# Exponentials on VectorE beside a long convolution: a new rule for when the planner gives VectorE a unit of softmax

## The chip, the cores and the metric

The kernel runs on one core of one Trainium2 chip. The metric is the device time of one execution in microseconds; of several executions the median is given.

## The reference

Two independent branches are computed and laid side by side in the last dimension. Everything is in bf16, S = 2048 positions, D = 640 channels.

```python
# branch A, out[..., 0:640]
k_shift = sum over t of k_pad[:, t:t+S, :] * shift_k[:, ks-1-t]     # ks = 4
kv = k_shift * v
y  = causal convolution of kv with ssm_k along S (written as rfft, product, irfft)
y  = y + kv * ssm_D
a  = q * y
# branch B, out[..., 640:1280]
q, k, v = split(x @ wqkv) into 32 heads of 20
p = softmax(q @ k.T * 20 ** -0.5)
b = (p @ v) joined over heads @ wo
```

Branch B holds 32 heads x 2048 x 2048 = 134 million exponentials. Branch A holds a convolution of length 2048 in each of 640 channels, and after it three elementwise operations for each output: kv times ssm_D, plus y, times q.

## The kernel before

**Units.** The scores are made transposed, keys on the 128 partitions and 512 queries along the free dimension. One such 128x512 tile of one head is a *unit*; there are 2048 of them (NU), and four units (four heads, one block of keys) make a *block*. TensorE writes the scores of a unit into one of eight PSUM banks (`S_task`, the matmul in line 568), an engine takes the exponential and writes bf16 into a slot of `P_sb`, and TensorE multiplies by V (`PV_task`, line 646), block after block in order. The row sums come out of a column of ones in V.

**Two engines take exponentials.** ScalarE takes groups of three and two units in turn, one ACTIVATE for each group (line 585, `EXP_task`), from banks 0 to 4. VectorE can take one more unit after each group (`VEXP_task`, `vexp_iter`): its scores go to the bank called AUX, and five VectorE instructions make the exponential from integer and polynomial steps: lines 615, 618, 620, 623 and 625. The first step is put out at once, the other four wait in a list called `chain`, which holds two units at most. VectorE's units have four slots of `P_sb` of their own.

**A planner writes the order.** When the kernel is built, a loop (the `while nu[0] < NU` loop) walks through model time. It keeps a time `P.T` for each engine and a cost `c` for each instruction, and decides what TensorE does next: the next score group as soon as its banks come free, urgent work, a pair of PV blocks, a piece of convolution, other tasks, and, when nothing else can be put in, matmuls on zeros (`zeros`, line 317). Each engine then runs its instructions in the written order, and waits on semaphores. The planner's times exist only at build time: they settle the order, not the speed.

VectorE's list is filled at two places. `fill_dve(now)` runs at each turn of the loop and puts out steps as long as VectorE's model time is not past `now`:

```python
while P.T["dve"] <= now + 0.05 and dve_step(now):
```

and `P.gap` lets a VectorE instruction that would wait be preceded by such steps. `dve_step` serves `chain` first; only when it is empty does it serve the list `micro`, in which the VectorE work of branch A stands.

**Branch A in stages.** First `kv_iter` computes k_shift times v (118 steps on VectorE, lines 476, 485, 489 and 508) and stores kv to a scratch tensor in HBM. Then the convolution runs on TensorE as 40 block rows of 16 channels (`conv_iter`, line 869: 128 small matmuls each, 5120 in all). After each block row VectorE copies the result out of the bank MISC, splits off the rounding (lines 882, 883), TensorE adds shifted parts (line 890), and VectorE copies into `Y` (line 896). Five block rows make a *chunk* of 80 channels; there are eight chunks. When a chunk of the convolution is finished, `A_iter` is put on `micro`: it loads q and kv for the chunk, and does the three elementwise operations (line 913) for each of four parts h, 12 steps a chunk. Parts 0 and 1 are loaded at the start into two pairs of buffers; the loads of parts 2 and 3 are issued after the output of parts 0 and 1 has been sent from the same buffers. These transfers, the convolution's (four banks of rows of `kext`, `hk_load`, one load for a quarter of a block row, four ahead; and `kvx_load`), and the outputs are all issued on SyncE's queue (SP), in order.

**When VectorE may take a unit** is settled in `vec_at`, asked once for every ScalarE group. It refuses when two units are in `chain`, when VectorE's model time is over 1.1 us ahead, when the slot has not been read, when the AUX bank is not free, and by pace. During `kv_iter`, 0.9 steps per us counted from 60 us must have been done. Afterwards:

```python
elif micro and kv_done[0] < a_at[0] + 12 * (now - a_at[1]) / (20 if conv_over else 50):
    return False
elif not conv_over and conv_b < 40 * (n - CONV0) / (NU - CONVE - CONV0):
    return False
```

So as long as steps of `A_iter` are left, they must have kept a pace of 12 in 50 us from the end of the chunk, or VectorE gets no unit. The second condition asks that the convolution keep pace with the units: `conv_b` block rows begun, n units begun, 40 block rows at n = 2008.

## Time and profile before

| | |
|---|---|
| median of 5 executions | 901.09 us (900.52 to 903.14) |
| profiled execution, its own time | 903.14 us |
| its span, first to last instruction | 901.3 us |
| ScalarE (ACT) busy | 882.7 us, 98% |
| TensorE (PE) busy | 866.6 us, 96% |
| VectorE (DVE) busy | 610.0 us, 68% |
| units taken by ScalarE, by VectorE | 1940, 108 |

The page names engines PE (TensorE matmuls), PEld (its weight loads), DVE (VectorE), ACT (ScalarE), POOL (GpSimd) and SP (SyncE, which here only issues transfers). A group's line gives source line, engine, operation, output and input, shapes, how many (x), then busy time in us and the mean ns of one, then the engine's idle time just before them and what ended it. Sums of steps are made against the profiled execution; 1.84 us of its own time lie outside the span.

The stages by time: projections and the start of attention to about 75 us; `kv_iter` beside attention to about 207 us; the convolution's matmuls from 233.5 to 852.7 us, with the eight chunk ends (last copy into `Y`) at 312.7, 394.7, 469.1, 547.3, 624.9, 708.4, 786.7 and 855.7 us; the last exponential ends at 892.55 us and the rest is the end of branch B.

### The profile page before, as it was taken

How to read it: one execution, taken by the hardware profiler on the slowest of the kernel's cores; microseconds unless marked ns; L12 is line 12 of the kernel's file. 1: busy time of each engine (PE TensorE's matmuls, PEld its weight loads, DVE VectorE, ACT ScalarE, POOL GpSimd, SP SyncE). 2: the span in 40 equal slices, each digit the busy share in tenths (PEclk: the TensorE clock that was granted, in tenths of full speed). 3: DMA queues.
4: the chain of work that ended last, by engine and by line, in shares of the span. 5: the costliest groups of instructions: out<-in, count | busy, mean ns of one | idle time of the engine just before them, and what ended most of it. 6: DMA issues, size and time to landing. Idle time of an engine off the chain costs nothing.

```text
span 901.3 us, 26290 instructions
## 1 busy us (share of the span) xinstructions
PE 866.6 (96%) x11636; PEld 406.2 (45%) x11636; DVE 610.0 (68%) x1142; ACT 882.7 (98%) x788; POOL 51.7 (6%) x75
## 2 busy tenths in 40 slices
PE   9999999999999999999999999999999999999997
PEld 5433322222455445455555455454545545455522
DVE  3477677677777777767775775777577475857741
ACT  6999999999999999999999999999999999999996
POOL 3001224332000000000000000000000000000000
PEclk9999999999999999999999999999999999999999
DMA  9512367766867668858866875895687677658410
GB/s 288 171 41 72 119 195 231 219 192 130 183 157 169 162 141 179 176 159 183 185 159 167 199 167 146 182 208 140 143 201 157 183 173 176 169 144 203 109 30 30
DMA packets 175517, 144.98 MB, mean 161 GB/s; under 512 B 138769, under 2 KB 150155, under 8 KB 175403
## 3 DMA queue, kind: packets, MB, share of 16 engines
q1 hardware_dynamic: 164027, 129.60, 59.1%
q0 software_dynamic: 9920, 13.33, 5.7%
q8 instruction: 91, 1.49, 0.7%
q10 hardware_dynamic: 1456, 0.37, 0.2%
q14 instruction: 23, 0.19, 0.1%
HBM read 124.67 MB, written 21.09 MB: 162 GB/s over the span
## 4 chain that ended last, share of the span: by engine, by line
ACT 96%; PE 4%; DVE 0%; issue 0%; DVEq 0%
ACT P_sb L585 96%; PE PS L392 1%; PE PS L568 1%; PE PS L317 1%; PE PS L447 0%; PE PS L646 0%; PE PS L368 0%; PE PS L749 0%; DVE P_sb L793 0%; DVE OT_sb L655 0%; DVEq L1182 0%; PE PS L670 0%; PE PS L772 0%; DVE V_sb L453 0%; DVE KT L380 0%
## 5 line engine op out<-in xcount | busy, mean ns | idle before, releaser
L585 ACT ACTIVATE P_sb<-PS 128x1024 bf16<-128x1024 f32 (+1 forms) x780 | 878.1, 1414 | 4.4 <-PE PS L568 4.2
L568 PE MATMUL PS<-QT,KT 20*128 20x512 bf16 x2048 | 303.8, 385 | 27.4 <-ACT P_sb L585 23.1
L869 PE MATMUL PS<-R 128*128 128x128 bf16 (+15 forms) x5120 | 249.6, 193 | 1.1 <-DVE R L896 1.1
L869 PEld LDWEIGHTS PS<-R 128*128 128x128 bf16 x5120 | 199.1, 96 | 105.5 <-issue 105.4
L568 PEld LDWEIGHTS PS<-QT,KT 20*128 20x128 bf16 x2048 | 74.8, 91 | 223.3 <-ACT P_sb L585 166.9
L646 PE MATMUL PS<-P_sb,V_sb 128*21 128x512 bf16 x2048 | 155.0, 383 | 0.9 <-DVE P_sb L625 0.7
L615 DVE TENSOR_SCALAR XI<-PS 128x512 int32<-128x512 f32 x108 | 74.6, 691 | 73.4 <-PE PS L568 72.0
L625 DVE SCALAR_TENSOR_TENSOR P_sb<-XZ,XI 128x512 uint16<-128x512 f32 x108 | 74.6, 690 | 3.0
L618 DVE SCALAR_TENSOR_TENSOR XZ<-XI 128x512 f32<-128x512 uint16 x108 | 74.3, 688 | 2.1
L317 PE MATMUL PS<-Zt 128*128 128x512 bf16 x252 | 74.7, 392 | 1.0 <-DVE Zt L311 1.0
L620 DVE SCALAR_TENSOR_TENSOR XZ<-XZ,XI 128x512 f32<-128x512 f32 x108 | 74.1, 686 | 1.6
L476 DVE TENSOR_TENSOR R<-R 128x640 bf16<-128x640 bf16 (+1 forms) x96 | 57.8, 602 | 2.0 <-DMA R<-in_A_v_dram 0.2
L646 PEld LDWEIGHTS PS<-P_sb,V_sb 128*21 128x21 bf16 x2048 | 30.8, 89 | 56.5 <-issue 48.3
L192 POOL DMA_DIRECT2D kvm_scratch<-R x64 | 43.9, 692 | 143.7 <-DVE R L508 142.3
L623 DVE TENSOR_SCALAR XI<-XI 128x512 int16<-128x512 int16 x108 | 49.3, 456 | 2.0
L655 DVE CAST OT_sb<-PS 128x512 bf16<-128x512 f32 x32 | 22.1, 689 | 39.2 <-PE PS L646 39.2
L380 DVE CAST QT<-PS 128x512 bf16<-128x512 f32 (+1 forms) x32 | 21.9, 684 | 36.8 <-PE PS L392 36.8
L380 DVE CAST KT<-PS 128x512 bf16<-128x512 f32 (+1 forms) x32 | 21.7, 678 | 29.5 <-PE PS L392 29.4
L392 PE MATMUL PS<-xT,R 128*20 128x512 bf16 (+2 forms) x660 | 41.5, 381 | 0.0
L392 PE MATMUL PS<-xT,WQ 128*20 128x512 bf16 (+1 forms) x660 | 40.3, 374 | 0.0
L882 DVE CAST ZH<-PS 128x256 bf16<-128x256 f32 x40 | 16.9, 423 | 22.4 <-PE PS L869 22.2
L453 DVE CAST V_sb<-PS 128x160 bf16<-128x160 f32 (+1 forms) x48 | 18.4, 383 | 17.2 <-PE PS L447 16.5
(51 smaller groups left out, 359.6 us busy)
## 6 DMA issues: line engine op xcount, KB each, us to landing
R<-kext_scratch SPq DMA_DIRECT2D x640, 132.0 KB, 3.1
kvm_scratch<-R POOLq DMA_DIRECT2D x64, 160.0 KB, 5.5
R<-kvm_scratch SPq DMA_DIRECT2D x32, 320.0 KB, 5.1
R<-in_A_k_dram SPq DMA_DIRECT2D x15, 640.0 KB, 3.8
kext_scratch<-in_A_ssm_k_dram POOLq DMA_DIRECT2D x1, 2560.0 KB, 13.5
R<-in_A_v_dram SPq DMA_DIRECT2D x16, 160.0 KB, 4.3
kv_scratch<-R SPq DMA_DIRECT2D x16, 160.0 KB, 5.0
R<-in_A_q_dram SPq DMA_DIRECT2D x32, 80.0 KB, 2.5
```

The costliest lines, as they stand in the source:

```text
L317: P.op("pe", lambda e: e.matmul(bank[bk], Zt, zrhs, start=start, stop=start, skip_group_check=True), reads=[b_Zt], writes=[bkb[bk]], tok=s ...
L392: ins = e.matmul(bank[bk][32 * i:32 * i + DH, 0:n], Wt[:, cc, off + i * DH:off + (i + 1) * DH], xT[:, cc, x0:x0 + n], start=(cc == 0), sto ...
L476: P.op("dve", lambda e: e.tensor_tensor(o, a, b, op), reads=reads, writes=writes, c=c)
L568: ins = e.matmul(bank[b], KT[32 * u:32 * u + DH, g, kb * 128:(kb + 1) * 128], QT[32 * u:32 * u + DH, qs(qc, g), :], start=True, stop=True, ...
L585: P.op("act", lambda e: e.activation(P_sb[:, s0:s0 + k, :], PS[:, b0 * 512:(b0 + k) * 512].rearrange("p (u q) -> p u q", u=k), ACT.Exp, sc ...
L615: step(lambda e: e.tensor_scalar(XI, bank[bk], scale * 1.4426950408889634 * w, 127.0 * w, op0=ALU.mult, op1=ALU.add), [bkb[bk]], [bi])
L618: step(lambda e: e.scalar_tensor_tensor(XZ, u, w * c2 / c3, u, op0=ALU.add, op1=ALU.mult), [bi], [bz])
L620: step(lambda e: e.scalar_tensor_tensor(XZ, XZ, w * w * c1 / c3, u, op0=ALU.add, op1=ALU.mult), [bi, bz], [bz])
L623: step(lambda e: e.tensor_scalar(hi, hi, 128.0, None, op0=ALU.mult), [bi], [bi])
L625: step(lambda e: e.scalar_tensor_tensor(P_sb[:, slot[n], :].bitcast(U16), XZ, 128.0 * c3 / w ** 3, hi, op0=ALU.mult, op1=ALU.add), [bi, bz ...
L646: ins = e.matmul(bank[OBANK][32 * u:32 * u + DH + 1, :], V_sb[:, kb, 4 * g + u, :], P_sb[:, slot[4 * b + u], :], start=(kb == 0), stop=(kb ...
L869: P.op("pe", lambda e, o=o, lhsT=lhsT, rhs=rhs, st=st, last=last: e.matmul(o, lhsT, rhs, start=st, stop=last, skip_group_check=True), read ...
```

## The change

The buffers for branch A's elementwise part become four pairs, and `A_iter` issues all four pairs of loads at its start. The pace of 12 steps in 50 us is replaced by a count: `a_at` is now the number of steps that would be done if all finished chunks were, and `vec_at` refuses a unit only when more than BACK = 12 steps are outstanding, or when the convolution is over and any are. `fill_dve` puts out steps up to 0.35 us ahead of VectorE's model time. Two costs in the planner's book change: the fourth step of a VectorE unit (line 623) from 0.7 to 0.48, and a step of `A_iter` from 0.43 to 0.33. No instruction of the kernel is changed in itself; what changes is order, and how many units go to which engine. The region R in SBUF, in which these buffers lie, is as large as before, since its other use (24,960 elements a partition) is larger than the new need (23,808).

```diff
+BACK = 12
...
-        ph1 = NHK * HK_E + 2 * KVX_E + 2 * Y_E + 4 * AST_E
+        ph1 = NHK * HK_E + 2 * KVX_E + 2 * Y_E + 8 * AST_E
...
-        Aq = [carve(AST_E).rearrange("p (t c) -> p t c", t=4) for _ in range(2)]
-        Akv = [carve(AST_E).rearrange("p (t c) -> p t c", t=4) for _ in range(2)]
+        Aq = [carve(AST_E).rearrange("p (t c) -> p t c", t=4) for _ in range(4)]
+        Akv = [carve(AST_E).rearrange("p (t c) -> p t c", t=4) for _ in range(4)]
...
-            def step(fn, reads, writes):
-                P.op("dve", fn, reads=reads, writes=writes, c=0.7)
+            def step(fn, reads, writes, c=0.7):
+                P.op("dve", fn, reads=reads, writes=writes, c=c)
...
-            step(lambda e: e.tensor_scalar(hi, hi, 128.0, None, op0=ALU.mult), [bi], [bi])
+            step(lambda e: e.tensor_scalar(hi, hi, 128.0, None, op0=ALU.mult), [bi], [bi], 0.48)
...
         def A_load(B, h):
-            i = h % 2
+            i = h
...
         def A_iter(B):
-            A_load(B, 0)
-            A_load(B, 1)
+            for h in range(4):
+                A_load(B, h)
...
-                P.op("dve", lambda e: e.tensor_tensor(o, a, b, op), reads=reads, writes=writes, c=0.43)
+                P.op("dve", lambda e: e.tensor_tensor(o, a, b, op), reads=reads, writes=writes, c=0.33)
...
-                if h + 2 < 4:
-                    A_load(B, h + 2)
...
-            while P.T["dve"] <= now + 0.05 and dve_step(now):
+            while P.T["dve"] <= now + 0.35 and dve_step(now):
...
-        kv_done, a_at = [0], [0, 0.0]
+        kv_done, kv_base, a_at = [0], [0], [0]
...
-            elif micro and kv_done[0] < a_at[0] + 12 * (now - a_at[1]) / (20 if conv_over else 50):
+            elif micro and (conv_over or a_at[0] - kv_done[0] > BACK):
+
                 return False
...
-            if not micro:
+            if not micro and not kv_over:
                 kv_over = True
+            if kv_over and not kv_base[0]:
+                kv_base[0] = kv_done[0]
...
-                            a_at[:] = [kv_done[0], P.T["pe"]]
+                            a_at[0] = max(a_at[0], kv_base[0]) + 12
```

## The prediction

> **What bounds the kernel.** I read the chain that ended last first, then the costliest groups, then waits, then stages.

> ```profile
> ACT 96%; PE 4%; DVE 0%; issue 0%; DVEq 0%
> ...
> L585 ACT ACTIVATE P_sb<-PS 128x1024 bf16<-128x1024 f32 (+1 forms) x780 | 878.1, 1414 | 4.4 <-PE PS L568 4.2
> ...
> L615 DVE TENSOR_SCALAR XI<-PS 128x512 int32<-128x512 f32 x108 | 74.6, 691 | 73.4 <-PE PS L568 72.0
> ```

> ScalarE's exponentials are the whole path, and it idles 4.4 us before them. So the time is 1940 units at 878.1 / 1940 = **0.453 us** each, plus the two ends. A unit moved to VectorE saves 0.453 us as long as TensorE keeps up. On VectorE the five groups of lines 615 to 625 are busy 346.9 us for 108 units: 3.21 us each. VectorE has idle time, and much of it is before line 615: it waits for the scores of a unit that the planner has given it late. The question is how many more units the new rules give it.

> The stages show where units are missing. Rows are stretch, its length, line 615's busy time and count, then TensorE's clock, DMA share and GB/s:

> ```profile
> 395.00:445.00 50.00, 4.14 (x6) 1.00 0.79 169
> 445.00:469.00 24.00, 3.94 (x6) 1.00 0.84 194
> ...
> 708.00:758.00 50.00, 2.77 (x4) 1.00 0.75 177
> 758.00:787.00 29.00, 4.84 (x7) 1.00 0.74 178
> ```

> The longer stretches run from a chunk's end to its last step of line 913, where the pace rule holds. Over the seven of them before 855 us (341 us) VectorE takes 40 units and is busy 229 us, 67%; over the eight others from 225 us (289 us) 63 units, busy 217.5 us, 75%. VectorE's order after the chunk end at 394.7 us shows the mechanism:

> ```profile
> 398.93 0.69 DVE L625 SCALAR_TENSOR_TENSOR P_sb<-XZ,XI 128x512 uint16<-128x512 f32 x1
> 404.47 0.69 DVE L655 CAST OT_sb<-PS 128x512 bf16<-128x512 f32 x1 [4.84 <-PE PS L646]
> ...
> 408.76 0.32 DVE L913 TENSOR_TENSOR R<-R,Dbc 128x320 bf16<-128x320 bf16 x1
> ...
> 411.64 0.69 DVE L615 TENSOR_SCALAR XI<-PS 128x512 int32<-128x512 f32 x1 [1.25 <-PE PS L568]
> ```

> Units are refused from the chunk's end, the queued ones drain, only then are loads issued (402.18 us on SP's queue), and no unit starts for 18.8 us (392.80 to 411.64). Parts 2 and 3 repeat it: loads at 414.49, next step at 424.80.

> **Loads and buffers.** The same 64 transfers, four pairs in a row instead of two. Two pairs took SP from 402.18 to 404.26 us, so four take 4.2 us, ahead of the convolution's loads, which stand up to three quarter rows ahead; a block row comes every 15.6 us (607.9 us for 39), so three quarters are 11.7 us. Hidden. Removed are SP's waits for the output to leave a buffer, 40.8 us in 16; these hide nothing today, since line 869 waits 1.1 us in all. Price of both: 0; if the cover were gone, 4.2 us a chunk on TensorE. A new load of part 3 can wait behind the previous chunk's output only where two chunks run back to back; about 2.6 us (40.8 / 16), under the same cover.

> **Pace rule.** If the seven stretches ran like the others, VectorE would be busy 0.753 x 341 = 257 us instead of 229: 28 us, or +8.6 units.

> **Looking ahead, and the booked costs.** Today a step is put out only when the book shows VectorE free, and the loop turns only once per piece of TensorE work: 0.39 us for a score group, 0.61 for a PV pair, 1.26 for a projection. A step that comes due inside a piece waits half of it. With these pieces filling roughly 33%, 18% and 5% of the stage, that is 0.06 + 0.055 + 0.03 = 0.15 us; less the 0.05 allowed, 0.1 a step, 0.5 a unit. The booking of line 623 adds 0.22. So up to 0.7 of the 1.13 us that VectorE idles per unit in the free stretches (71.5 us / 63) is the book's, not the chip's.

> [...] a step starts 0.72 us after the one it reads from (busy 0.69), and 0.61 after one it doesn't. [...] But the idle time before lines 618 to 625 is only 8.7 us for 108 units; what the lookahead shortens lies ahead of line 615, in the book. I take the book, at part.

> **Sum for 225 to 855 us.** VectorE is busy 447 us there, 103 units x 3.21 = 331 and 116 other. In about 620 us at a busy share y it takes (620 y - 116) / 3.21 units: y = 0.753 gives 109 (+6), 0.84 gives 126 (+23), 0.92 gives 141 (+38). Copies that wait for TensorE in VectorE's own order stay (lines 380, 882, 896, 655 and 715 wait 90 us here), so I take 0.84. Before 225 us units are rationed by `kv_iter`'s pace: by 95 us 19 steps are done where 31 are asked. A quicker book catches up late: +3 (0 to +8). The **convolution's pace** takes some back. At 855.7 us, when it ends, ScalarE has (892.55 - 855.7) / 0.453 = 81 units left, so n is about 1967 where 2008 is allowed: room for 41 units, less 2.2 (1 / 0.453) for each us that it ends later. Steps put out ahead stand before the two VectorE copies of each block row; 0.15 us a row, 6 us in all, leave 28. TensorE can carry it: it is busy 96%, but 100 matmuls on zeros lie in this stage (about 26 us), and 14 us of gaps. I take -4. Together **+22 units, -10.0 us**: 893.1 for an execution like the profiled one, **891** against the median of 901.09 (901.1 - 10.0). The last chunk's steps ended at 874.4 us, 18 us before ScalarE did; today's end is unchanged, and up to 24 steps (24 x 0.35 = 8.4 us) still fit.

> **Rivals.** *More*: the convolution keeps its speed and VectorE reaches 0.9: +31 to +48 units, 879 to 887. For it: decisions in the free stretches are frequent, one per ScalarE group (1.13 us). Against: the 90 us of copies.
> *Starved steps*: `chain` is served first, and if it is never empty the steps of a chunk wait until the next one ends; units are then refused until a chunk's loads and 12 steps are through, about 6 us (402.18 to 408.76) and 4. Seven times 10 us are 70 us, 22 units at worst; half of that leaves +4 to +15: 894 to 899.
> *Nothing*: the copies and TensorE's order fix VectorE's share: 899.3 to 902.9.
> *Slower*: TensorE waits in order for a VectorE unit. One place shows the price; rows are TensorE's busy time in 1 us stretches with its clock, then ScalarE:

> ```profile
> 94.00:95.00 1.00, 0.72 (x7) 1.00 0.00 0
> 95.00:96.00 1.00, 0.58 (x6) 0.70 0.00 0
> 96.00:97.00 1.00, 1.00 (x14) 0.50 0.78 271
> ...
> 99.14 4.62 ACT L585 ACTIVATE P_sb<-PS 128x1536 bf16<-128x1536 f32 x4 [1.52 <-PE PS L568]
> ```

> PV waited 0.70 us for line 625, a projection then ran at half clock (2.35 us instead of 1.26), ScalarE lost 1.52 us. [...] Here gaps of 0.70 and 0.44 us within 3 us were enough, [...] by the row 1.5 us each. It happened once with 108 units. From seven (10.0 / 1.52) it eats the gain; with ten to fourteen more the time is 906 to 912. Against it: with the looser book VectorE reached line 615 before its scores nearly always (72 us of waiting), and that margin shrinks but does not vanish.

> **How the numbers follow.** +16 to +30 units, 887.5 to 894: 0.54. More: 0.12. Starved: 0.21. Nothing: 0.05. Slower: 0.08. This kernel's measurement can tell about 0.2%, 899.3 to 902.9. Faster 0.54 + 0.12 + 0.21 = 0.87, same 0.05, slower 0.08. The range 883 to 899 leaves out about 0.07 below and 0.13 above; it holds the likeliest case whole.

> **What would show it.** Line 615 counts about 130, and line 585 some nine ACTIVATEs fewer; VectorE's share from 225 to 855 us rises from 71% to about 84%; no stretch of 15 us without a unit follows a chunk's end; loads of branch A come in fours; idle time before line 615 falls under 0.4 us each. If ScalarE's idle time before line 585 rises above 10 us, the slower rival is at work; if line 913 comes in blocks of 12 or more right after the next chunk's end, the starved one. I am wrong if the count moves by under ten, or if the time doesn't follow it at 0.45 us a unit.

## The result, and the profile after

The changed kernel takes 889.88 us in the median of 25 executions (887.68 to 905.77), against 901.08 before (900.28 to 903.32); the ratio is **0.9888, interval 0.9876 to 0.9901**. I had forecast 891. The median holds some executions in which TensorE's clock fell: of 26 listed with their clock, 17 had 0.998 or more and lie between 887.7 and 892.1 us, nine had 0.979 to 0.996 and lie between 892.3 and 905.8. Line numbers in the changed kernel are one higher from here on (615 is 616).

The page of the changed kernel, span 887.5 us, own time 889.33: the chain by engine, then ScalarE's exponentials and the first step of a VectorE unit, with busy time, mean ns and idle time before.

```profile
ACT 92%; PE 4%; DMA 1%; SPq 1%; DVE 0%; issue 0%; DVEq 0%
...
L586 ACT ACTIVATE P_sb<-PS 128x1024 bf16<-128x1024 f32 (+1 forms) x769 | 865.2, 1416 | 3.7 <-PE PS L569 3.6
...
L616 DVE TENSOR_SCALAR XI<-PS 128x512 int32<-128x512 f32 x137 | 94.7, 691 | 33.3 <-PE PS L569 29.0
```

VectorE takes 137 units instead of 108, ScalarE 1911 in 769 ACTIVATEs instead of 780, and ScalarE is busy 12.9 us less (878.1 to 865.2): 0.445 us a unit. ScalarE still has the path, and waits no more than before. Idle time ahead of line 616 fell from 0.68 to 0.24 us each. New in the chain are a transfer and SP's queue, 1% each.

All engines in the stage from 225 to 855 us; busy time and count of PE, PEld, DVE, ACT, POOL, then clock, DMA share, GB/s:

```profile
225.00:855.00 630.00, 611.32 (x9045) 317.58 (x9042) 529.88 (x979) 629.25 (x558) 0.00 (x0) 1.00 0.70 166
```

VectorE is busy 529.9 of 630 us, 84.1%, where it was 446.8. But the stage is not even. Line 616 by stretches (busy time, count):

```profile
294.00:368.00 74.00, 11.06 (x16) 1.00 0.67 170
368.00:384.00 16.00, 0.81 (x2) 1.00 0.67 156
384.00:449.00 65.00, 10.26 (x15) 1.00 0.82 184
449.00:464.00 15.00, 0.86 (x2) 1.00 0.38 103
```

and VectorE's order in the second of them:

```profile
368.17 0.69 DVE L616 TENSOR_SCALAR XI<-PS 128x512 int32<-128x512 f32 x1
...
372.31 0.42 DVE L897 CAST R<-PS 128x256 bf16<-128x256 f32 x1
...
375.94 0.32 DVE L914 TENSOR_TENSOR R<-R,Dbc 128x320 bf16<-128x320 bf16 x1
...
381.40 0.69 DVE L914 TENSOR_TENSOR R<-R 128x320 bf16<-128x320 bf16 x2
383.88 0.69 DVE L616 TENSOR_SCALAR XI<-PS 128x512 int32<-128x512 f32 x1 [1.79 <-PE PS L569]
```

The chunk that ended at 294.0 us gets none of its 12 steps until the next one ends at 372.3. Then units are refused, the steps run in one block, and 15.7 us pass without a new unit (368.17 to 383.88). The same happens at each later chunk end. Between the blocks a unit starts every 4.3 to 4.6 us (65 / 15 and 74 / 16) where the mean of this stage was 6.2 before (630 / 102).

### The profile page after: what moved, and what is told of

Its sections match the earlier page's. It is cut to its first block, busy times and chain, and to the rows that moved or that the text cites. A ratio compares the mean times of both kernels' runs of the same rounds, so it can differ in the third digit from the quotient of the medians.

```text
span 887.5 us, 26392 instructions
## 1 busy us (share of the span) xinstructions
PE 850.1 (96%) x11594; PEld 402.5 (45%) x11594; DVE 697.8 (79%) x1287; ACT 869.7 (98%) x777; POOL 51.7 (6%) x75
## 4 chain that ended last, share of the span: by engine, by line
ACT 92%; PE 4%; DMA 1%; SPq 1%; DVE 0%; issue 0%; DVEq 0%
ACT P_sb L586 92%; PE PS L393 1%; DMA R<-kvm_scratch 1%; SPq L193 1%; PE PS L569 1%; DMA R<-kext_scratch 1%; PE PS L318 1%; PE PS L750 0%; PE PS L647 0%; PE PS L448 0%; PE PS L369 0%; DVE P_sb L794 0%; PE PS L870 0%; DVE OT_sb L656 0%; DVEq L1184 0%
## 5 line engine op out<-in xcount | busy, mean ns | idle before, releaser
L586 ACT ACTIVATE P_sb<-PS 128x1024 bf16<-128x1024 f32 (+1 forms) x769 | 865.2, 1416 | 3.7 <-PE PS L569 3.6
L569 PE MATMUL PS<-QT,KT 20*128 20x512 bf16 x2048 | 299.0, 384 | 28.8 <-ACT P_sb L586 24.6
L616 DVE TENSOR_SCALAR XI<-PS 128x512 int32<-128x512 f32 x137 | 94.7, 691 | 33.3 <-PE PS L569 29.0
L626 DVE SCALAR_TENSOR_TENSOR P_sb<-XZ,XI 128x512 uint16<-128x512 f32 x137 | 94.6, 690 | 4.0
L621 DVE SCALAR_TENSOR_TENSOR XZ<-XZ,XI 128x512 f32<-128x512 f32 x137 | 94.2, 687 | 2.6
L619 DVE SCALAR_TENSOR_TENSOR XZ<-XI 128x512 f32<-128x512 uint16 x137 | 93.8, 685 | 1.4
L624 DVE TENSOR_SCALAR XI<-XI 128x512 int16<-128x512 int16 x137 | 62.9, 459 | 3.5
L318 PE MATMUL PS<-Zt 128*128 128x512 bf16 x210 | 63.2, 392 | 1.0 <-DVE Zt L312 1.0
L448 PE MATMUL PS<-R,xT 128*128 128x160 bf16 (+1 forms) x240 | 29.1, 256 | 0.1
## 6 DMA issues: line engine op xcount, KB each, us to landing
kext_scratch<-in_A_ssm_k_dram POOLq DMA_DIRECT2D x1, 2560.0 KB, 13.9
```

What stands on the lines that cost most here:

```text
L318: P.op("pe", lambda e: e.matmul(bank[bk], Zt, zrhs, start=start, stop=start, skip_group_check=True), reads=[b_Zt], writes=[bkb[bk]], tok=s ...
L569: ins = e.matmul(bank[b], KT[32 * u:32 * u + DH, g, kb * 128:(kb + 1) * 128], QT[32 * u:32 * u + DH, qs(qc, g), :], start=True, stop=True, ...
L586: P.op("act", lambda e: e.activation(P_sb[:, s0:s0 + k, :], PS[:, b0 * 512:(b0 + k) * 512].rearrange("p (u q) -> p u q", u=k), ACT.Exp, sc ...
L616: step(lambda e: e.tensor_scalar(XI, bank[bk], scale * 1.4426950408889634 * w, 127.0 * w, op0=ALU.mult, op1=ALU.add), [bkb[bk]], [bi])
L619: step(lambda e: e.scalar_tensor_tensor(XZ, u, w * c2 / c3, u, op0=ALU.add, op1=ALU.mult), [bi], [bz])
L621: step(lambda e: e.scalar_tensor_tensor(XZ, XZ, w * w * c1 / c3, u, op0=ALU.add, op1=ALU.mult), [bi, bz], [bz])
```

## The experiments

**Which part brought the units.** My theory was that the time follows the number of units, and that the planner's book (look-ahead and booked costs) gives most of them; the rival was that only the pace rule counts (+8.6 units). The book alone, on the kernel before:

```diff
-            while P.T["dve"] <= now + 0.05 and dve_step(now):
+            while P.T["dve"] <= now + 0.35 and dve_step(now):
...
-            step(lambda e: e.tensor_scalar(hi, hi, 128.0, None, op0=ALU.mult), [bi], [bi])
+            step(lambda e: e.tensor_scalar(hi, hi, 128.0, None, op0=ALU.mult), [bi], [bi], 0.48)
...
-                P.op("dve", lambda e: e.tensor_tensor(o, a, b, op), reads=reads, writes=writes, c=0.43)
+                P.op("dve", lambda e: e.tensor_tensor(o, a, b, op), reads=reads, writes=writes, c=0.33)
```

> Kernel before with the look-ahead of 0.35 us and the booked costs (0.48 and 0.33) alone; old pace rule, two pairs of buffers. As planned, VectorE takes 134 units. Theory (units decide, and the planner's book gives them): 26 more units at 0.453 us are 11.8 us, so about 889.3 us. Rival [...]: within 2 us of before, 899 to 902 us. A third reading, that the trains of loads on SP's queue cause the spread of the changed kernel, expects this one's executions to lie within 4 us of each other.

Measured 890.68 us (890.09 to 897.71, four executions, ratio 0.9893, interval 0.9852 to 0.9935). Its page:

```profile
L585 ACT ACTIVATE P_sb<-PS 128x1024 bf16<-128x1024 f32 (+1 forms) x770 | 866.6, 1419 | 3.0 <-PE PS L568 2.8
...
L615 DVE TENSOR_SCALAR XI<-PS 128x512 int32<-128x512 f32 x134 | 92.5, 690 | 36.6 <-PE PS L568 33.4
```

26 of the 29 new units come from three numbers in the book. The third reading fails in one of its four executions, 7 us off (clock 0.990), in a kernel whose loads of branch A go out in fours and twos: a fall of the clock doesn't need the trains of eight. The look-ahead alone, the first of the three edits:

> Kernel before with the look-ahead of 0.35 us alone; as planned, 121 units. Theory (units decide): 13 units, 5.9 us less than before's undisturbed executions of 900.6, about 894.7 us. [...]

Measured 895.79 us (895.10 to 895.89), 121 units, ratio 0.9948 (0.9933 to 0.9962): 4.8 us for 13 units against executions of before on that chip at 900.56, where 5.9 were forecast. The rest, alone:

```diff
+BACK = 12
...
-            elif micro and kv_done[0] < a_at[0] + 12 * (now - a_at[1]) / (20 if conv_over else 50):
+            elif micro and (conv_over or a_at[0] - kv_done[0] > BACK):
...
+            for h in range(4):
+                A_load(B, h)
```

(with the four pairs of buffers and the counters that belong to it)

> Kernel before with the count in place of the pace rule and four pairs of buffers alone; old look-ahead and booked costs. As planned, 117 units. Theory (units decide): 9 more units, 4.1 us less, about 897.0 us. The rival [...] (this part carries the gain) expects most of the 11 us: 890 to 893 us.

Measured 902.29 us (898.17 to 915.59): both missed. It has its 117 units, and its lowest execution, 898.17, is near the 897.0 that they ask for; but 14 of 22 executions have a clock of 0.977 to 0.995, up to 17 us longer. So the count in place of the pace rule, with its buffers, is worth +9 units alone and +3 on top of the book, and brings something that costs more. What that is comes after one test of the units.

Is it the units at all, or does the new order save waits? One more refusal in the changed kernel:

```diff
+CAP = 108
...
-            if len(chain) > 1 or not 140 < n < NU - 30 or P.T["dve"] > now + 1.1:
+            if vn[0] >= CAP * (n - 140) / (NU - 170) or len(chain) > 1 or not 140 < n < NU - 30 or P.T["dve"] > now + 1.1:
```

> The changed kernel with one more refusal: VectorE gets no unit beyond an even share of 108 over the run. Everything else of the change stays. Theory (units alone decide): same count as before, 900 to 902 us. Rival (the new order saves waits of its own): under 898 us. Rival (the new order costs waits that the extra units hide): over 904 us.

Measured 901.53 us (900.44 to 912.40; one of 12 over 903), ratio 1.0008 (0.9985 to 1.0031). With the old count the new order has the old time, within 0.3%. The units decide.

**What halves the clock.** An execution of pace_only that took 915.05 us was profiled. Its order around 720 us, transfers, TensorE and ScalarE:

```profile
719.66 0.51 SPq L193 DMA_DIRECT2D R<-in_A_q_dram  x1
...
720.20 0.51 SPq L193 DMA_DIRECT2D R<-kv_scratch  x1
...
720.76 2.51 SPq L193 DMA_DIRECT2D R<-kext_scratch  x4
...
725.83 0.29 PE L870 MATMUL PS<-R 128*128 128x128 bf16 x2 [1.38 <-DMA R<-kext_scratch]
...
726.49 2.37 ACT L586 ACTIVATE P_sb<-PS 128x1536 bf16<-128x1536 f32 x2 [1.07 <-PE PS L569]
```

Eight loads of branch A stand in a row on SP's queue from 716.30 us; the convolution's rows, issued behind them, land late; TensorE waits 1.38 us in order at line 870. Then TensorE by stretches (busy, count, clock, DMA share, GB/s):

```profile
720.00:727.00 7.00, 5.60 (x95) 1.00 0.97 191
727.00:740.00 13.00, 13.00 (x97) 0.50 0.92 183
740.00:755.00 15.00, 15.00 (x167) 0.50 0.39 110
755.00:764.00 9.00, 9.00 (x56) 0.50 0.61 117
764.00:780.00 16.00, 15.90 (x233) 0.98 0.60 147
```

The clock is halved for 37.5 us by the trace's record, and ScalarE, which idles 17.5 us in this execution where 2.8 is usual, loses about 15 us. The theory is that the trains of eight loads make the convolution's loads late; the rival, that TensorE has too little work by itself. The trains alone are not enough: cap108 puts its loads out in trains of eight too, two of them 13.9 us apart (370.65 and 384.50 us), and only one of its 12 executions has a lower clock. Here the train began 14.2 us after the one before it (702.08 us). First I took the loads off SP's queue:

```diff
-            P.dmas("sp", [(Aq[i], ap(q2, dims, o)), (Akv[i], ap(kvd, dims, o))], d_aq[i],
+            P.dmas("pool", [(Aq[i], ap(q2, dims, o)), (Akv[i], ap(kvd, dims, o))], d_aq[i],
```

> The changed kernel with the loads of branch A's elementwise part issued on GpSimd's queue instead of SP's; as planned, 138 units. Theory (trains of eight loads on SP's queue delay the convolution's loads, TensorE waits, and in some executions its clock is halved): all executions within 3 us, granted clock 0.998 or above, median about 887.5 us. Rival (TensorE's work is too thin by itself, whatever the queue): executions spread over 5 us or more with clocks of 0.98 to 0.995 as in the changed kernel, whose executions go from 887.7 to over 899 us.

Measured 899.09 us (894.23 to 909.85), every one of 20 executions with a clock under 0.998: worse than the changed kernel. The timeline says why it was a poor test:

```profile
215.91 0.75 POOL L193 DMA_DIRECT2D R<-in_A_q_dram  x1
...
221.13 13.27 SPq L193 DMA_DIRECT2D R<-kext_scratch  x16
...
228.38 0.37 PE L870 MATMUL PS<-R 128*128 128x128 bf16 x2 [7.05 <-DMA R<-kvm_scratch]
...
230.30 1.02 ACT L586 ACTIVATE P_sb<-PS 128x1024 bf16<-128x1024 f32 x1 [7.28 <-PE PS L569]
```

On GpSimd's queue nothing stood ahead of the first chunk's loads, so they were issued from 213 us, among the first loads of the convolution, of which one then came 7 us late. In the changed kernel SP's order holds them back to 370.86 us. The clock is halved again behind a late load of the convolution (7.05 us of waiting, then 44.4 us at half clock), but this doesn't test the trains. That the early transfers delayed the convolution's is what the order suggests; it was not separated.

Better was to leave the queue and give the convolution's loads more lead, one bank of rows more, in the changed kernel and in pace_only:

```diff
-NHK = 4
+NHK = 5
```

> The count and the four pairs of buffers alone (old look-ahead and booked costs), with five banks of convolution rows; as planned, 116 units. With four banks half the executions lay between 908 and 916 us. Theory (late loads): none over 905 us, median 897 to 899 us (8 units at 0.453 are 3.6 us). Rival (want of work): still a good share over 905 us.

Measured 897.40 us (896.59 to 899.74), ratio 0.9970 (0.9961 to 0.9979), 116 units. None of nine executions has a clock under 0.998, where 14 of 22 had with four banks. ScalarE's row with four banks (the execution above), then with five:

```profile
L586 ACT ACTIVATE P_sb<-PS 128x1024 bf16<-128x1024 f32 (+1 forms) x777 | 876.3, 1409 | 17.5 <-PE PS L569 17.2
```

```profile
L586 ACT ACTIVATE P_sb<-PS 128x1024 bf16<-128x1024 f32 (+1 forms) x777 | 874.5, 1421 | 2.8 <-PE PS L569 2.7
```

For the count alone this shows late loads as the cause, as far as one chip can be set against another: the two ran on different chips, with 116 and 117 units. That it was the trains that made them late was not separated. In the changed kernel itself:

> The changed kernel with five banks of convolution rows instead of four (NHK = 5), so the convolution's loads are issued one quarter row (about 3.9 us) earlier. As planned, VectorE takes the same 137 units. Theory (trains of eight loads on SP's queue make the convolution's loads late, TensorE waits in order, its clock is halved for tens of us in some executions): TensorE's waits for kext go to nothing, granted clock 0.998 or above in nearly all executions, median 887 to 888.5 us, all under 892. Rival (the clock is halved for want of work on TensorE, not for late loads): a tail of executions from 892 to 906 us as in the changed kernel.

Measured 889.10 us (888.06 to 889.52), ratio 0.9871 (0.9859 to 0.9884), no wait for kext left (one of 0.5 us for `kvm_scratch` is). Four executions are few against a tail of one in three, so both kernels ran once more side by side:

> The changed kernel with five banks once more, for more executions beside the changed kernel on the same chip. Theory (late loads): again 887.5 to 890 us, none over 892. Rival (four executions were too few to see the tail): a third of them over 892, as with four banks.

> The changed kernel itself, for comparison on the same chip: 888 to 890 us in about two of three executions, the others 892 to 906 with a granted clock under 0.998.

Five banks: 889.07 us (888.33 to 903.82, one of four with a clock of 0.978). Changed kernel: 891.93 us (888.99 to 912.62, four of seven under 0.998). Together one of eight against 13 of 33. The direction is the theory's, but chance alone would give one or none of eight about one time in seven, and one execution at 903.82 went against "none over 892". There is a second cause that five banks don't remove, or the lead is still short in some executions. No trace of such an execution was taken, and this stays open.

**What the four pairs of buffers are for.** In the changed kernel, two pairs as before, part h + 2 loaded behind the output of part h:

```diff
-            i = h
+            i = h % 2
...
-            for h in range(4):
-                A_load(B, h)
+            A_load(B, 0)
+            A_load(B, 1)
...
+                if h + 2 < 4:
+                    A_load(B, h + 2)
```

> The changed kernel with two pairs of buffers instead of four, loads of parts 2 and 3 issued after the outputs of parts 0 and 1 as before; as planned, 132 units. Theory of the prediction (the buffers are worth nothing on the path): 24 units more than before, 10.9 us, about 890 us. Rival (with the count in place of the pace rule the last chunk's steps start so late that, load after output in the same buffers, they end behind attention): over 900 us, with ScalarE's last exponential at about 880 us and line 913 ending behind it.

Measured 905.93 us (902.83 to 919.05), ratio 1.0052 (1.0038 to 1.0067): slower than before with 24 more units. The end of VectorE's order:

```profile
891.08 0.33 DVE L914 TENSOR_TENSOR R<-R,Dbc 128x320 bf16<-128x320 bf16 x1 [4.01 <-DMA R<-kv_scratch]
...
894.53 0.33 DVE L914 TENSOR_TENSOR R<-R,Dbc 128x320 bf16<-128x320 bf16 x1 [2.40 <-DMA R<-kv_scratch]
894.89 0.68 DVE L914 TENSOR_TENSOR R<-R 128x320 bf16<-128x320 bf16 x2
895.49 0.68 DVE L656 CAST OT_sb<-PS 128x512 bf16<-128x512 f32 x1
```

and ScalarE's:

```profile
879.15 1.78 ACT L586 ACTIVATE P_sb<-PS 128x1024 bf16<-128x1024 f32 x2
901.16 1.08 ACT L792 ACTIVATE P_sb<-PS 128x512 bf16<-128x512 f32 x2 [20.23 <-PE PS L750]
```

Exponentials end at 880.9 us. But the copy that attention's last head group needs (line 656) stands in VectorE's order behind the 24 steps of the last two chunks, and parts 2 and 3 of each wait for an output to leave and a load to land; TensorE waits 13.3 us for that copy, and ScalarE 20.2 us where the changed kernel has 4.8. The rival was right.

**A version that beats both.** First try: five banks, every third VectorE step for branch A when its data is there (its loads issued at the chunk's end), look-ahead 0.5, pace of `kv_iter` 0.8.

```diff
-NHK = 4
+NHK = 5
...
-KVPACE, CONV0, CONVE = 0.9, 620, 40
+KVPACE, CONV0, CONVE = 0.8, 620, 40
...
-            while P.T["dve"] <= now + 0.35 and dve_step(now):
+            while P.T["dve"] <= now + 0.5 and dve_step(now):
...
+            turn[0] += 1
-            if chain:
+            if chain and not (kv_over and micro and turn[0] % 3 == 0 and micro[0][1] not in (None, "end") and
+                              not (micro[0][1] and P.ready("dve", micro[0][1]) + 2.0 > max(P.T["dve"], now))):
...
+                            for h in range(4):
+                                A_load(conv_next[1] * 16 // CH, h)
...
```

> A version meant to beat both: the changed kernel with five banks, every third VectorE step given to branch A's elementwise part when its data is there (its loads issued at the chunk's end), look-ahead 0.5 us, and the pace asked of branch A's first part 0.8 instead of 0.9. As planned, 147 units. Theory: 10 units more than the changed kernel, 4.5 us, so 883 to 884 us, with a tail only if loads are late. If VectorE's fuller queue makes TensorE wait: over 886 us.

Measured 893.91 us (888.09 to 896.02): 147 units, but a clock of 0.987 to 0.996 in all six executions. Its trace has TensorE waiting 2.3 us for the first load of the convolution at 231.9 us, and a halved clock from there: a score group (line 569) takes 0.61 us at 232.68, where one at 228.64 took 0.39. The granted clock of this execution, 0.988 over 891.5 us, makes about 21 us at half clock in all. So the pace went back to 0.9, and the first block row waits for its loads to be safely there:

```diff
-                if conv and not conv_over and misc_at() <= now + 0.03 and P.ready("pe", conv_reads(conv_b)) + 1.5 <= now:
+                if conv and not conv_over and misc_at() <= now + 0.03 and P.ready("pe", conv_reads(conv_b)) + (1.5 if conv_b else 6.0) <= now:
```

> Second try at a version that beats both: the changed kernel with five banks of convolution rows, every third VectorE step for branch A's elementwise part when its data is there (loads issued at the chunk's end), look-ahead 0.5 us, the pace of branch A's first part as before, and the first block row of the convolution begun only when its loads are planned to have landed 6 us earlier. As planned, 144 units. Theory (units decide once no load is late): 7 units more than the changed kernel, 3.2 us, so 884.5 to 886 us, clock 0.998 or above, no execution over 890. If a start of the convolution before its loads was not what halved the clock in the version before: again 893 to 896 us.

Measured **884.51 us** (884.14 to 885.32, four executions), ratio 0.9814 (0.9799 to 0.9829). Its page:

```profile
L586 ACT ACTIVATE P_sb<-PS 128x1536 bf16<-128x1536 f32 (+1 forms) x766 | 861.7, 1437 | 2.8 <-PE PS L569 2.7
...
L616 DVE TENSOR_SCALAR XI<-PS 128x512 int32<-128x512 f32 x144 | 99.4, 690 | 37.7 <-PE PS L569 34.1
```

It is 16.1 us under 900.6, where the kernel before lies at full clock, for 36 units: 0.447 us each. Its trains of loads begin at least 55 us apart (777.08 and 832.22), and the trace has no wait for a load of the convolution. Which of its edits brought how much was not taken apart, nor which of the last two mended the clock.

## Why the prediction was right or wrong

**The bound and the price were right.** 0.453 us a unit was forecast; 0.445 by ScalarE's busy time, 0.447 from before to the best version. By the clock of whole executions the single steps gave less: 4.8 us for 13 units (0.37), and 11.3 for 29 in the changed kernel at full clock (0.39). cap108 shows that at the old count nothing else in the change moves the median.

**The choice of the book was right.** The instructions on VectorE are as long as before (691, 685, 687, 459 and 690 ns; before 691, 688, 686, 456 and 690), and a step still starts 0.72 us after the one it reads from (374.10 to 374.82) and 0.61 after one it doesn't (368.17 to 368.78), so nothing was gained on the chip by issuing early. What was gained is that the planner, believing VectorE free sooner, put in more. The busy share of 0.84 that I took was 84.1%.

**The count was low, 22 for 29.** The term before 225 us was right (9 units there for 6, the +3). My 103 units in the stage counted one twice at the edge of a stretch: it is 102, and 127 start there now, where the share of 0.84 asked for 126. The pace rule alone, +8.6, is the +9 of pace_only, but only +3 on top of the book. The term that failed is the convolution's pace, -4. It rested on the two copies of a block row coming later behind early steps; but the time from the end of one block row's matmuls to the start of the next was 3.9 us after for 4.1 before. Attention advanced faster, so the convolution also began sooner (221.5 us for 233.5), and ended at 838.3 with n at about 1960 of 2008 (ScalarE's last exponential ends at 878.3, and 40.0 / 0.453 is 88 units). Its pace never bound.

**The starved rival came true in its mechanism and not in its time.** `chain` is served first, and every chunk's steps wait for the next chunk's end, as it said; I had called a stretch of 15 us without a unit gone. There are six of 14.8 to 20.2 us between 368 and 775 us. In the stretches that hold these pauses and the last one VectorE is busy 74% (85.3 of 116 us), in between 86% (444.6 of 514). That the two come to the 84% I had taken for an even stage is luck. The better version removes most of it: after 255 us its longest pause is 13.6 us.

**The price of loads and buffers, 0, was wrong in both parts.** The cover that I named, three quarter rows or 11.7 us, is a mean. Behind outputs that wait for VectorE, with two chunks back to back, the loads of one more chunk were enough to make TensorE wait in some executions. In the profiled execution, eight loads from 383.61 us follow eight from 370.86, then TensorE and ScalarE wait:

```profile
397.03 0.63 PE L870 MATMUL PS<-R 128*128 128x128 bf16 x9 [0.88 <-DMA R<-kext_scratch]
...
398.58 3.71 ACT L586 ACTIVATE P_sb<-PS 128x1536 bf16<-128x1536 f32 x3 [0.75 <-PE PS L569]
```

Such waits are the likeliest source of the tail up to 906 us; no execution of the changed kernel with a fallen clock was traced. They are not what the median lacks. At full clock the executions went from 900.6 to 889.3, 11.3 us where 29 units ask for 13.1, and with five banks, without this wait, they lie at 889.1. I can't place the missing 1.8 us. And the buffers, which I took for a convenience, decide whether the new rule can be used at all: with two pairs the end came about 15 us later (20.2 us of waiting where 4.8 is usual). I had asked what hides the load trains in the middle, not what stands behind the last chunk's steps in VectorE's order. My "up to 24 steps still fit" counted steps and not their loads.

**The slower rival had too low a price and the wrong releaser.** In pace_only a wait of TensorE in order of 1.38 us was followed by 37.5 us at half clock; but what TensorE waits for in the changed kernel is a load of the convolution and not a VectorE unit. The 1.5 us that I read is ScalarE's wait alone: of the kernel before, the executions with a clock of 0.998, that of the profiled one with its halved 3.41 us, take 903.0 to 903.3 us, the others 900.1 to 901.5. Among its matmuls' waits in the changed kernel there is none for line 626, and the halved clock at 96 us is gone from the trace.

## What to carry to other kernels

Where a planner writes the order at build time, its cost table and its notion of "free" are a resource like a queue: here three numbers were worth 26 of 29 units and no instruction got faster. Price a shared queue's cover at its worst place, behind instructions that themselves wait, and not at its mean; and when work is allowed to fall behind, look at what stands behind it in the order at the end. A change that wins in the median can bring a tail of longer executions: read the clock of every execution, not only of the profiled one.

## What the runs showed of the hardware

In these traces the busy share around a gap tells more than its length. I cut those of the kernel before and of the changed kernel into stretches of 3.413 us, the length of that shortest span in the record, set by the moments at which the recorded clock changed. In the kernel before, gaps of 0.70 and 0.44 us lie together in the stretch ahead of the halving (91.99 to 95.40 us), in which TensorE is busy 67%; in every other stretch at full clock from 11 to 890 us it is busy 82% or more. In the changed kernel no stretch from 8 to 885 us is under 70%, and the clock stays at 1.00: the wait of 0.88 us at 397.03 us, longer than either gap, lies in a stretch that is 74% busy. In pace_only TensorE is busy 1.62 of the last 3 us ahead of the halving (724 to 727). The 37.5 us at half clock cost ScalarE about 15 us there (17.5 us idle where 2.8 is usual).
